# Attention in the layers' PSUM banks, scan turns placed ahead, and transposed copies written in runs of four words

## The chip, the cores and the metric

One core of one Trainium2 chip runs the whole program. The metric is the device time of one launch in microseconds (us): 1198.31 us is the median of 3 runs (1196.89 to 1199.21). Engines are named as in the profile: PE is TensorE (its weight loads are PEld), DVE is VectorE, ACT is ScalarE, POOL is GpSimd, SP is SyncE, which issues nearly all DMAs. Each engine works through its own queue in order. SBUF is the on-chip memory that all of them use; PSUM is the small memory into which PE writes, 8 banks of 128 partitions x 512 fp32 words.

## The reference

The input goes through a gated linear recurrence (called attention here) and then two feed-forward layers.

```python
# q, k, v, a_re, a_im: (4, 8, 768, 48); a is scaled to magnitude at most 0.999
for t in range(S):
    S_re, S_im = a_re*S_re - a_im*S_im + outer(k[t], v[t]), a_re*S_im + a_im*S_re
    y[t] = q[t] @ S_re
x = y as (3072 tokens, 384)
h = x @ w_in;   x = (h * clip(h + 3, 0, 6) / 6) @ w_out          # layer 1, d_ff 2048
h = x @ w_in2;  x = (max(h, 0) + alpha * min(h, 0)) @ w_out2     # layer 2, d_ff 2048
```

The weights arrive as 64-bit floats and are turned into pairs of fp32r words on the chip (DVE and ACT, lines 73 to 77, 293 and 294); each product of a layer is three fp32r matmuls.

## The kernel before

**Groups.** A group n is one batch and 256 of its 768 positions: two chunks (g = 0, 1) of 128 positions, all 8 heads. There are 12 groups, three per batch. Each has a normalisation (`norm_ops`), a scan (`scan_ops`), an attention (`attn_ops`, that is `chunk_ops` for each chunk) and `split_x`, which hands its result to the layers.

**Scan.** The cumulative products of the complex gates. DVE first runs along 8 steps within each of 128 partitions (lines 396 to 398). `totals` then copies the last step (ACT, tile `tot`, line 409), turns it with two PE transposes into the PSUM tile `ptt` (line 412) and copies it out to `bt` (ACT, line 413). On `bt` DVE runs four rounds of four small operations (429 to 432) and some twenty tiny ones (447 to 485). `back` turns the result with two transposes (`pe`, line 492) and one ACT copy (`EL`, line 495). DVE multiplies it in (508 to 510), and last come the scaled keys `Kt` and queries, which lie in place of `A` (518).

**Attention of a chunk.** Eight heads share a chunk, and its keys and queries, 96 values for each position, are turned so that the 96 are on the partitions. `tr` does that in four calls: `Kt` half 0, `Kt` half 1, queries half 0, half 1. A call is four PE transposes (line 566) into the PSUM tile `pt`, and one ACT copy (line 567) from there to `KT` or `QT`. Position 8t + j of a head lies at transpose j, column t, so the copy before reads 512 words in a row in PSUM and writes them 8 words apart:

```python
nc.scalar.copy(
    dst.rearrange("p h (t j) -> p j (h t)", j=J)[:, 4 * half : 4 * half + 4], pt[:D2])
```

`scores(i)` is one product for each of four heads (eight PE records of line 589) into `ps`, and one DVE multiply by the mask into `PT` (590). `outputs` adds the two products of four pairs of heads in `py` (624, 626), ACT copies it to `ys` (628), and six SP DMAs carry it to `xr`. `update` carries the state on: `pu` (599), a small product `gx` (601), then DVE and ACT on `W`.

**PSUM.** `ps1` has one buffer each of the tags `pt`, `ps` and `py`. `pt` serves `totals`, `back`, all `tr` calls and `gx`; `ps` serves both `scores` and `pu`. `psh` has two buffers of the tag `ph` (lines 649 on), in which the layers' first products land; `psf` has the three accumulators of the second products. That is all 8 banks.

**Layers.** `ffn` runs a layer over one or two groups, 16 blocks of 128 inner features each: `ain` (`ph`, line 658), `gate` (ACT and DVE, 670 to 680, result `gs`) and `bout` (`acc`, line 695).

**What sets the order.** The program text is produced by a list of positions written by hand: each step has a place on a made-up time axis (`tl.at`, `tl.stream`), and the operations of scan, attention and layers are interleaved by it. Group 0's attention has positions 46 to 56 and the first pass over group 0 starts at 58; group 1's attention has 110 to 122, between the end of that pass and the pass that starts at 122; group 2's scan has 152 to 190. The framework's scheduler then fills each engine's queue: among the instructions that are ready by its own timing model it takes the one that stands first in the text, and a tile gets a buffer when the one before it in that buffer is released. The queues are fixed before the program runs. `tc.high_priority(offset=n)` makes the instructions in it count as standing n places earlier.

Of the kernel before, what the change touches and what calls it, by code (L numbers as in the profile page):

```python
# [9 lines left out]
F32 = mybir.dt.float32  # L10
# [7 lines left out]

P = 128
NB = 1  # L20
WACT = 4
LAG = {1: 2, 2: 5}
NW = 15
# [2 lines left out]
C = 128  # L26
G = 2
GT = G * C
TB, J = 16, 8
# [190 lines left out]
def recurrence_ffn_kernel(ctx: ExitStack, tc, al, qkl, vl, w1, w2, alpha, q, k, v, a_re, a_im, out):  # L220
# [8 lines left out]
    D2 = 2 * D  # L229
# [10 lines left out]
    psh = main.enter_context(tc.tile_pool(name="psh", bufs=2, space=PSUM))  # L240
# [86 lines left out]
    ps1 = att.enter_context(tc.tile_pool(name="ps1", bufs=1, space=PSUM))  # L327
# [10 lines left out]
    def grp(n):  # L338
        return divmod(n, NG)
# [44 lines left out]
    def scan_ops(n):  # L384
# [4 lines left out]
        ops = []  # L389
# [15 lines left out]
        b2 = lp.tile([P, 2, H, TB], F32, tag="b2", name=f"b2_{n}")  # L405
        E = lp.tile([P, 2, H, TB], F32, tag="E", name=f"E{n}")

        def totals():
            nc.scalar.copy(tot[:, :, :, :D].rearrange("p c g d -> p g c d"), A[:, J - 1])
            pt = ps1.tile([P, 2, P], F32, tag="pt", name=f"ptt{n}")  # L410
            for c in range(2):
                nc.tensor.transpose(pt[:, c], tot[:, c].rearrange("p g d -> p (g d)"), ident)
            nc.scalar.copy(bt.rearrange("p c h t -> p c (h t)"), pt)

        ops.append(totals)
        for r in range(4):
            w = 1 << r
            xv = bt.rearrange("p c h (k w) -> p c (h k) w", w=2 * w)
# [24 lines left out]
        ph, phn = phi[n % 2], phi[(n + 1) % 2]  # L443
# [50 lines left out]
                )  # L494
            nc.scalar.copy(EL, pe_)

        ops.append(back)
        late = [lambda: V.scalar_tensor_tensor(gam, n2, SC, y1, op0=ALU.mult, op1=ALU.mult)]
        if cp_ < NG - 1:
            late += turn(phn[0:64], ph, 64)  # L500
# [3 lines left out]
        for g in range(G):  # L504
            X = A[:, :, g]
            x = X.rearrange("p j c d -> p j (c d)").unsqueeze(1).broadcast_to([P, 2, J, 2 * D])
# [4 lines left out]

        Kt = lp.tile([P, J, G, 2, D], F32, tag="Kt", name=f"Kt{n}", bufs=NB)
        Q_t[n], K_t[n] = A, Kt
# [27 lines left out]
    def attn_ops(n):  # L541
        xr = xr_t[n] = lp.tile([P, KT, GT], F32, tag="xr", name=f"xr{n}", bufs=2)
        return [op for g in range(G) for op in chunk_ops(n, g, xr)]
# [9 lines left out]
    def chunk_ops(n, g, xr):  # L553
        b, cp_ = grp(n)
        c = G * cp_ + g
        Qt, Kt, V = Q_t[n], K_t[n], V_t[n]
        QT = lp.tile([D2, H, C], F32, tag="QT", name=f"QT{n}_{g}", bufs=2)
        KTr = lp.tile([D2, H, C], F32, tag="KT", name=f"KT{n}_{g}")
        KN = lp.tile([P, H, D2], F32, tag="KN", name=f"KN{n}_{g}")
        PT = [lp.tile([P, 4, C], F32, tag="PT", name=f"PT{n}_{g}_{i}", bufs=2) for i in range(2)]  # L560
        ops = []

        def tr(src, dst, half):
            pt = ps1.tile([P, 4, P], F32, tag="pt", name=f"pt{n}_{g}_{half}")
            for jj in range(4):
                nc.tensor.transpose(pt[:D2, jj], src[:, 4 * half + jj, g].rearrange("p c d -> p (c d)"), ident)  # L566
            nc.scalar.copy(  # L567
                dst.rearrange("p h (t j) -> p j (h t)", j=J)[:, 4 * half : 4 * half + 4], pt[:D2]
            )

        def natural():
            if c < NCH - 1:
                for h in range(H):
                    nc.sync.dma_start(
                        KN[:, h],
                        Kt[TB * h : TB * (h + 1), :, g].rearrange("p j c d -> p j (c d)"),
                    )

        def kt0():
            natural()  # L580
            tr(Kt, KTr, 0)

        ops += [kt0, lambda: tr(Kt, KTr, 1), lambda: tr(Qt, QT, 0), lambda: tr(Qt, QT, 1)]

        def scores(i):
            ps = ps1.tile([P, 4, C], F32, tag="ps", name=f"ps{n}_{g}_{i}")
            for hh in range(4):
                h = 4 * i + hh
                nc.tensor.matmul(ps[:, hh], lhsT=KTr[:, h], rhs=QT[:, h], start=True, stop=True)  # L589
            nc.vector.tensor_mul(PT[i], ps, mask.unsqueeze(1).broadcast_to([P, 4, C]))  # L590

        ops += [lambda: scores(0), lambda: scores(1)]

        def update():
            if c == NCH - 1:
                return
            pu = ps1.tile([P, H, D], F32, tag="ps", name=f"pu{n}_{g}")
            for h in range(H):
                nc.tensor.matmul(pu[:D2, h], lhsT=KN[:, h], rhs=V[:, g, h], start=True, stop=True)  # L599
            gx = ps1.tile([P, H], F32, tag="pt", name=f"gx{n}_{g}")  # L600
            nc.tensor.matmul(
                gx[:D2], lhsT=sel[:, g].rearrange("p c d -> p (c d)"), rhs=gam_t[n], start=True, stop=True
            )
            W = lp.tile([D2, H, D], F32, tag="W", name=f"W{n}_{g}", bufs=2)
            gb = gx[:D2].unsqueeze(2).broadcast_to([D2, H, D])
            if c == 0:
                nc.scalar.copy(W, pu[:D2])
            else:
                nc.vector.tensor_add(W, W_t[n, g], pu[:D2])
            if n < WACT:  # L610
                gs_ = lp.tile([D2, H], F32, tag="gsb", name=f"gsb{n}_{g}")
                nc.scalar.copy(gs_, gx[:D2])
                for h in range(H):
                    nc.scalar.activation(W[:, h], W[:, h], AF.Copy, scale=gs_[:, h : h + 1])
            else:
                nc.vector.tensor_mul(W, W, gb)
            W_t[(n, 1) if g == 0 else (n + 1, 0)] = W

        def outputs():
            for hp in range(H // 2):  # L620
                for par in range(2):
                    h = 2 * hp + par
                    o = py[64 * par : 64 * par + D, hp]
                    nc.tensor.matmul(o, lhsT=V[:, g, h], rhs=PT[h // 4][:, h % 4], start=True, stop=(c == 0))  # L624
                    if c > 0:
                        nc.tensor.matmul(o, lhsT=W_t[n, g][:, h], rhs=QT[:, h], start=False, stop=True)  # L626
            ys = lp.tile([P, 4, C], F32, tag="ys", name=f"ys{n}_{g}")
            nc.scalar.copy(ys, py)
            tk = slice(g * C, (g + 1) * C)
            for par in range(2):  # L630
                nc.sync.dma_start(xr[D * par : D * (par + 1), :, tk], ys[64 * par : 64 * par + D, 0:3])
            for par, e0, kk, p0, m in ((0, 0, 0, 96, 32), (0, 32, 1, 96, 16), (1, 0, 1, 112, 16), (1, 16, 2, 96, 32)):
                nc.sync.dma_start(xr[p0 : p0 + m, kk, tk], ys[64 * par + e0 : 64 * par + e0 + m, 3])

        ops += [outputs, update]
        return ops
# [85 lines left out]
    def group(n, norm, scan, attn, split):  # L722
        tl.at(max(norm[0] - 8, 0.0), lambda: load_a(n))
        tl.stream(*norm, lambda: norm_ops(n))
        tl.at(scan[0] if n else 0.5, lambda: load_qk(n))
        tl.stream(*scan, lambda: scan_ops(n))
        tl.at(attn[0] - 6, lambda: load_v(n))
        tl.stream(*attn, lambda: attn_ops(n))
        tl.at(split, lambda: split_x(n))
# [13 lines left out]
    for m in range(2, NGRP // 2):  # L743
        if m + 1 < NGRP // 2:
            n = 2 * m + 2
# [103 lines left out]
```

## Time and profile before

| | |
|---|---|
| median of 3 runs | 1198.31 us |
| the profiled execution | 1198.93 us, span 1197.2 us |
| PE busy | 1031.2 us (86%) in 5914 matmuls |
| DVE busy | 802.1 us (67%) |
| ACT busy | 615.3 us (51%) |
| mean granted PE clock | 0.975 of full |
| DMA | 194.60 MB moved |

Busy is the time in which an engine had an instruction under way, and a share of the whole span. The program has two parts: some 400 us in which groups 0 to 5 are prepared while the weights are decoded, then a regular pattern of two groups at a time.

### The profile page before, as it was taken

Reading aid. Unit: us, or ns where it says so; the run is one execution under the profiler, and the core shown is the slowest. Engines: PE = TensorE matmul, PEld = TensorE weight load, DVE = VectorE, ACT = ScalarE, POOL = GpSimd, SP = SyncE. Lnnn points to the kernel's source line nnn. Section 1 sums busy time; section 2 is a strip of 40 time slices with the busy share of each in tenths; the row PEclk is TensorE's granted clock in tenths of the full one; section 3 lists DMA queues with packets and bytes.
Section 4 is the critical chain, followed back from the end, with each engine's and each line's share of the span. In section 5 each row is a group of like instructions: output and inputs, shape, how many; then the busy total and the mean of one; then the engine's idle time right before and its main releaser. Section 6 shows DMA issues by size and latency. Waiting matters only on the chain.

```text
span 1197.2 us, 15796 instructions
## 1 busy us (share of the span) xinstructions
PE 1031.2 (86%) x5914; PEld 846.9 (71%) x5914; DVE 802.1 (67%) x1537; ACT 615.3 (51%) x1003; POOL 2.0 (0%) x13
## 2 busy tenths in 40 slices
PE   0026946979998789999999999999999999999997
PEld 0015935957787787777878778778788777788786
DVE  7985973999895586948738749559579375333432
ACT  5453634667665455755356564446554346432433
POOL 0000000000000000000000000000000000000000
PEclk9999876999999899999999999999999999999999
DMA  8642472476575675445534544543454344244430
GB/s 339 253 167 61 142 303 67 134 275 194 222 247 181 213 243 178 134 128 174 171 102 153 171 120 158 193 136 116 131 188 139 130 124 138 89 163 134 133 129 30
DMA packets 70500, 194.60 MB, mean 163 GB/s; under 512 B 29456, under 2 KB 38672, under 8 KB 70416
## 3 DMA queue, kind: packets, MB, share of 16 engines
q1 hardware_dynamic: 70272, 193.50, 48.6%
q8 instruction: 49, 0.80, 0.3%
q14 instruction: 35, 0.29, 0.1%
q10 hardware_dynamic: 144, 0.01, 0.0%
HBM read 158.08 MB, written 22.81 MB: 151 GB/s over the span
## 4 chain that ended last, share of the span: by engine, by line
PE 66%; DVE 16%; ACT 12%; DMA 3%; issue 2%; SPq 0%; DVEq 0%; ACTq 0%
PE ph L658 27%; PE acc L695 24%; PE ps L589 5%; PE pt L566 4%; ACT KT L567 4%; ACT QT L567 4%; PE pu L599 3%; PE py L624 2%; DVE w L294 2%; DVE wd L76 2%; DVE wd L77 2%; PE py L626 2%; DMA w<-wsd 1%; DVE gs L680 1%; DMA A<-in_al_dram 1%
## 5 line engine op out<-in xcount | busy, mean ns | idle before, releaser
L695 PE MATMUL acc<-gs,w 128*128 128x512 f32 (+1 forms) x2016 | 453.3, 366 | 7.2 <-ACT gs L679 4.8
L695 PEld LDWEIGHTS acc<-gs,w 128*128 128x128 f32 x2016 | 335.2, 188 | 69.2 <-ACT gs L679 7.3
L658 PE MATMUL ph<-xT,w 128*128 128x256 f32 (+1 forms) x1152 | 231.2, 348 | 20.9 <-ACT xT L550 14.9
L658 PE MATMUL ph<-xs,w 128*128 128x512 f32 x864 | 224.3, 401 | 3.2 <-DVE xs L704 2.5
L658 PEld LDWEIGHTS ph<-xT,w 128*128 128x128 f32 x1152 | 185.1, 197 | 50.8 <-ACT xT L550 16.0
L658 PEld LDWEIGHTS ph<-xs,w 128*128 128x128 f32 x864 | 158.3, 188 | 40.6 <-DVE xs L704 4.0
L679 ACT CAST gs<-r 128x512 fp32r<-128x512 f32 x192 | 119.7, 624 | 119.6 <-DVE r L671 71.6
L680 DVE TENSOR_TENSOR gs<-r,gs 128x512 fp32r<-128x512 f32 x192 | 132.0, 689 | 63.5 <-ACT gs L679 63.4
L678 DVE SCALAR_TENSOR_TENSOR r<-n,nal,r 128x512 f32<-128x512 f32 x96 | 71.9, 749 | 80.9 <-ACT n L675 80.5
L670 ACT ACTIVATE r<-ph 128x512 f32<-128x512 f32 x96 | 57.3, 597 | 129.2 <-PE ph L658 128.7
L671 DVE SCALAR_TENSOR_TENSOR r<-r,ph 128x512 f32<-128x512 f32 x96 | 65.7, 684 | 83.4 <-ACT r L670 82.9
L674 ACT ACTIVATE r<-ph 128x512 f32<-128x512 f32 x96 | 57.5, 599 | 83.9 <-PE ph L658 83.1
L567 ACT COPY KT<-pt 96x512 f32<-96x512 f32 x48 | 54.8, 1143 | 47.6 <-PE pt L566 39.4
L590 DVE TENSOR_TENSOR PT<-ps,mask 128x512 f32<-128x512 f32 x48 | 33.2, 692 | 62.7 <-PE ps L589 61.0
L589 PEld LDWEIGHTS ps<-QT,KT 96*128 96x128 f32 x384 | 54.5, 214 | 21.8 <-ACT QT L567 18.5
L589 PE MATMUL ps<-QT,KT 96*128 96x128 f32 x384 | 60.5, 307 | 10.7 <-ACT QT L567 9.7
L567 ACT COPY QT<-pt 96x512 f32<-96x512 f32 x48 | 54.8, 1142 | 21.5 <-PE pt L566 21.5
L566 PE MATMUL pt<-ident,Kt 128*96 128x128 f32 x192 | 33.1, 298 | 38.0 <-DVE Kt L518 30.5
L675 ACT ACTIVATE n<-ph 128x512 f32<-128x512 f32 x96 | 57.4, 598 | 0.0
L566 PEld LDWEIGHTS pt<-ident,Kt 128*96 128x96 f32 x192 | 22.6, 136 | 48.6 <-ACT wd L73 21.2
L566 PE MATMUL pt<-ident,A 128*96 128x128 f32 x192 | 33.8, 303 | 20.9 <-ACT QT L567 10.3
L566 PEld LDWEIGHTS pt<-ident,A 128*96 128x96 f32 x192 | 20.9, 135 | 38.7 <-ACT QT L567 19.0
(107 smaller groups left out, 1054.0 us busy)
## 6 DMA issues: line engine op xcount, KB each, us to landing
w<-wsd SPq DMA_DIRECT2D x139, 768.0 KB, 4.4
raw<-in_w_dram SPq DMA_DIRECT2D x32, 768.0 KB, 5.7
wsd<-w SPq DMA_DIRECT2D x23, 768.0 KB, 4.1
A<-in_al_dram SPq DMA_DIRECT2D x12, 768.0 KB, 4.6
qk<-in_qkl_dram SPq DMA_DIRECT2D x12, 768.0 KB, 5.4
KN<-Kt SPq DMA_DIRECT2D x160, 48.0 KB, 2.3
v<-in_vl_dram SPq DMA_DIRECT2D x12, 384.0 KB, 4.4
out_dram<-o SPq DMA_DIRECT2D x18, 256.0 KB, 3.2
```

The costliest lines, as they stand in the source:

```text
L566: nc.tensor.transpose(pt[:D2, jj], src[:, 4 * half + jj, g].rearrange("p c d -> p (c d)"), ident)
L567: nc.scalar.copy(dst.rearrange("p h (t j) -> p j (h t)", j=J)[:, 4 * half : 4 * half + 4], pt[:D2])
L589: nc.tensor.matmul(ps[:, hh], lhsT=KTr[:, h], rhs=QT[:, h], start=True, stop=True)
L658: nc.tensor.matmul(ph_, lhsT=w[:, wl, kk], rhs=x[:, xl, kk], start=(kk == 0 and wl == 0 and xl == 0), stop=(kk == KT - 1 and wl == 1),)
L670: nc.scalar.activation(r, ph_, AF.Relu, bias=0.5, scale=1.0 / 6.0)
L671: nc.vector.scalar_tensor_tensor(r, r, 1.0, ph_, op0=ALU.min, op1=ALU.mult)
L674: nc.scalar.activation(r, ph_, AF.Relu)
L675: nc.scalar.activation(neg, ph_, AF.Relu, scale=-1.0)
L678: nc.vector.scalar_tensor_tensor(r[:, k], neg[:, k], nal[:, ii : ii + 1], r[:, k], op0=ALU.mult, op1=ALU.add)
L679: nc.scalar.copy(gs[:, 0], r)
L680: nc.vector.tensor_sub(gs[:, 1], r, gs[:, 0].bitcast(F32))
L695: nc.tensor.matmul(acc, lhsT=w[:, wl, e * P : (e + 1) * P], rhs=gs[:, gl], start=(i == 0 and wl == 0 and gl == 0), stop=(i == NF - 1 and g ...
```

## The change

Three edits.

1. In `tr` and `scores` of groups 0 and 1, some tiles come from the layers' two `ph` buffers: of the four `tr` calls of a chunk the second and third (`Kt` half 1, queries half 0), and of the two `scores` the second. The others stay in `pt` and `ps`.
2. For groups 0 to 3, `totals` and `back` are emitted with an offset of 1000 places ahead.
3. In all groups the copy out of `pt` goes over its 512 words in another order: it writes four neighbouring words of `KT` or `QT` at a time and reads them from the four transposes, 128 words apart in PSUM. The words and their places are the same.

```diff
+URGE = 1000
@@ scan_ops
+        def urgent(f):
+            def g():
+                with tc.high_priority(offset=URGE):
+                    f()
+            return g if n < 4 else f
+
-        ops.append(totals)
+        ops.append(urgent(totals))
...
-        ops.append(back)
+        ops.append(urgent(back))
@@ chunk_ops
+        def bank(k, own, name):
+            pool, tag = (psh, "ph") if n < 2 and k else (ps1, own)
+            return pool.tile([P, 4, P], F32, tag=tag, name=name)
+
         def tr(src, dst, half):
-            pt = ps1.tile([P, 4, P], F32, tag="pt", name=f"pt{n}_{g}_{half}")
+            pt = bank((src is Kt) == half, "pt", f"pt{n}_{g}_{half}")
             for jj in range(4):
                 nc.tensor.transpose(pt[:D2, jj], src[:, 4 * half + jj, g].rearrange("p c d -> p (c d)"), ident)
             nc.scalar.copy(
-                dst.rearrange("p h (t j) -> p j (h t)", j=J)[:, 4 * half : 4 * half + 4], pt[:D2]
+                dst.rearrange("p h (t j) -> p (h t) j", j=J)[:, :, 4 * half : 4 * half + 4],
+                pt[:D2].rearrange("p j x -> p x j"),
             )
...
         def scores(i):
-            ps = ps1.tile([P, 4, C], F32, tag="ps", name=f"ps{n}_{g}_{i}")
+            ps = bank(i, "ps", f"ps{n}_{g}_{i}")
```

## Rows read from the trace of the kernel before

**Rows 1.** Page: busy us (share of the span) and instructions of each engine.

```profile
PE 1031.2 (86%) x5914; PEld 846.9 (71%) x5914; DVE 802.1 (67%) x1537; ACT 615.3 (51%) x1003; POOL 2.0 (0%) x13
```

**Rows 2.** Page: chain of waits that ended last, share of the span by line.

```profile
PE ph L658 27%; PE acc L695 24%; PE ps L589 5%; PE pt L566 4%; ACT KT L567 4%; ACT QT L567 4%; PE pu L599 3%; PE py L624 2%; DVE w L294 2%; DVE wd L76 2%; DVE wd L77 2%; PE py L626 2%; DMA w<-wsd 1%; DVE gs L680 1%; DMA A<-in_al_dram 1%
```

**Rows 3.** Stretches: length, busy PE, PEld, DVE, ACT, POOL, PE clock, DMA share, GB/s.

```profile
121.00:158.00 37.00, 34.99 (x279) 34.17 (x279) 35.10 (x62) 20.63 (x33) 0.00 (x0) 0.93 0.53 197
...
169.00:211.00 42.00, 26.67 (x171) 22.19 (x172) 15.53 (x48) 18.30 (x38) 0.00 (x0) 0.62 0.30 76
...
240.00:270.00 30.00, 22.62 (x118) 17.39 (x117) 29.64 (x44) 19.41 (x29) 0.00 (x0) 1.00 0.77 274
...
406.00:1197.00 791.00, 766.42 (x4131) 618.24 (x4130) 481.88 (x912) 395.21 (x636) 0.00 (x0) 1.00 0.44 143
```

**Rows 4.** Groups by line: count, busy us, mean ns, idle before and releasers.

```profile
L567 ACT COPY KT<-pt 96x512 f32<-96x512 f32 x48 | 54.8, 1143 | 47.6 <-PE pt L566 39.4 <-PE ps L589 8.0
L567 ACT COPY QT<-pt 96x512 f32<-96x512 f32 x48 | 54.8, 1142 | 21.5 <-PE pt L566 21.5
...
L628 ACT COPY ys<-py 128x512 f32<-128x512 f32 x24 | 14.1, 587 | 33.7 <-PE py L626 26.0 <-PE py L624 5.6 <-DMA w<-wsd 1.8
```

**Rows 5.** Groups by line: three small DVE operations.

```profile
L466 DVE TENSOR_TENSOR pq<-phi,u 64x32 f32<-64x32 f32 x20 | 3.7, 186 | 0.3
...
L447 DVE TENSOR_TENSOR sq<-bt 128x16 f32<-128x16 f32 x12 | 2.2, 182 | 0.2
...
L448 DVE TENSOR_TENSOR n<-sq 128x8 f32<-128x8 f32 x12 | 2.0, 164 | 0.3
```

**Rows 6.** Timeline, group 0: start, length, instruction, [idle before and releaser].

```profile
79.35 1.10 ACT L567 COPY KT<-pt 96x512 f32<-96x512 f32 x1 [1.51 <-PE pt L566]
...
80.50 1.08 PE L566 MATMUL pt<-ident,Kt 128*96 128x128 f32 x4 [1.19 <-ACT KT L567]
...
120.35 0.80 PE L658 MATMUL ph<-xT,w 128*128 128x256 f32 x2 [5.43 <-ACT xT L550]
```

**Rows 7.** Who waited for line 567, 78 to 205 us: us, times.

```profile
  PE pt L566: 13.3, 11
...
  PE ps L589: 4.6, 4
```

**Rows 8.** Waits of DVE, 78 to 205 us: total, times, longest.

```profile
DVE PT L590 <- PE ps L589: 31.6, 7, 8.0
DVE W L609 <- PE pu L599: 9.5, 3, 4.2
```

**Rows 9.** Timeline, totals of group 2 during group 1's attention.

```profile
173.31 0.37 ACT L409 COPY tot<-A 128x192 f32<-128x192 f32 x1
...
196.39 0.69 PE L412 MATMUL ptt<-ident,tot 128*128 128x128 f32 x2 [0.31 <-ACT gsb L612]
```

**Rows 10.** Who waited for line 567, 406 to 1197 us: us, times.

```profile
  PEld pt L566: 27.1, 39
  PE pt L566: 10.0, 29
  PEld ps L589: 9.6, 13
  PE ps L589: 3.9, 10
```

**Rows 11.** Who waited for line 567, 211 to 406 us: us, times.

```profile
  PEld pt L566: 6.0, 9
...
  PEld ps L589: 2.5, 4
```

**Rows 12.** Timeline, a chunk in the regular part.

```profile
601.54 1.18 PE L695 MATMUL acc<-gs,w 128*128 128x512 f32 x4
...
603.13 0.64 PE L566 MATMUL pt<-ident,Kt 128*96 128x128 f32 x4 [0.41 <-ACT KT L567]
```

**Rows 13.** Chain in order of time: start, length, engine and line, count.

```profile
472.89 2.10 PE acc L695 x9
```

## The prediction, on record before the result

> **What bounds the kernel now.** I read the page's busy shares first, then the chain of waits, the stretches, and who waits for the copies of line 567. PE is busy for 86% of the span and no other engine for more than 67% [rows 1], so PE is the likely bound, but not everywhere. From 406 us on it is: 766 of 791 us busy [rows 3], and the missing 25 us are small holes. Before that the bound changes hands. In 121 to 158 us DVE is busy 35.1 of 37 us, in 240 to 270 us 29.6 of 30 while PE has 7.4 us of holes; in 169 to 211 us neither is full (PE 26.7, DVE 15.5, ACT 18.3 of 42) [rows 3]. There one hands to the other: four transposes fill the single `pt`, PE stands for 1.19 us while ACT copies it out in 1.10 us, and only then come the next four [rows 6]. DVE, which has other work, stands in its queue behind the masks of `scores` for 31.6 us and behind `pu` for 9.5 us of the first two attentions [rows 8]. The 96 copies of line 567, 54.8 + 54.8 us, lie on the chain with 4% + 4% of the span, some 90 us [rows 2, 4]: nearly all of them. That overstates what they cost, since PE works during much of a copy; the holes before the instructions that wait are the better measure.
>
> **Edit 3, the copy's price.** Today it reads 512 words in a row and writes them 8 words apart, in 1143 ns; the copy of `py`, as long and in a row on both sides, takes 587 ns [rows 4]. So scattered writing costs 556 ns, 1.09 ns a word. The new copy writes runs of four and reads words 128 apart. No ACT row reads PSUM in steps, so I bound it. Below: if only the writing was dear, 587 ns, as `py`. Above: line 447 reads DVE words 16 apart, 16 of them in 182 ns, where 8 in a row take 164 (line 448) and 32 take 186 (line 466), which puts 16 at some 171 [rows 5]; 11 ns for 16 words is 0.7 ns a word, and 512 words at that price make 587 + 358 = 945 ns; at the price of the scattered write it stays at 1143 ns. A dearer read than that (1.7 us at twice the price) I keep as the far end. I take 600 ns: the two copies of rows 4 differ in nothing but the order of the writes, which shows where the time sits, and the one hint at dear reads is another engine on another memory.
>
> The Trainium skill, page "Advanced Engine Details and Errata", sections "SBUF Cachelines" and "PSUM Cachelines", says that SBUF wants at least two hits on a line of 16 bytes, and that PSUM's lines hold two fp32 words and should be used in neighbouring pairs. Its first half agrees with 1143 against 587 ns; its second half, which it states for matmuls, speaks against this edit, and no row here shows it for an ACT read. Taken for ACT as well, it leaves the copy about where it is, which is the first rival below.
>
> **Edit 3, from 406 us on.** PE's loads stand before `pt` and `ps` 39 + 13 times for 27.1 + 9.6 us, 0.71 us each; by the matmul rows, whose ends are modelled late, it is 10.0 + 3.9 us [rows 10]. One example says which is nearer: four products start at 601.54, the transposes behind them at 603.13 [rows 12]; nine such products in a row take 2.10 us [rows 13], four therefore 0.93, so of the 1.59 us between the starts some 0.66 are hole. A copy 0.55 us shorter takes most of it: 52 holes x 0.48 = 25 us. Bounds: 14 us (the matmul rows' sum) and 29 us (52 x 0.55). Next late are then the matmuls themselves.
>
> **Edit 3, from 211 to 406 us.** 9 + 4 such holes, 6.0 + 2.5 us [rows 11]: 13 x 0.4 = 5 us, between 2 and 7, less where DVE is what ends last.
>
> **Edits 1 and 3, the first two attentions.** PE stands 13.3 + 4.6 = 18 us for line 567 here [rows 7]. With `pt`, `ph`, `ph` for the first three calls the transposes no longer wait for a copy; only the fourth call waits for the first copy, and each chunk's `scores` for the last. With copies of 0.60 us that leaves about 0.7 us for each of the four chunks: 18 - 3 = 15 us. With copies of 1.1 us ACT needs 4.4 us for what PE turns in 4.3 (four times 1.08 [rows 6]), so some 1.2 us are left for each: 18 - 5 = 13 us, which is edit 1 by itself. The second bank for `scores` I count at nothing, since rows 7 hold only waits for line 567; it can only add. The waits that edit 1 adds are free: the first product of a layer needs a `ph` buffer, but it comes at 120.35 us and waits 5.43 us for `xT` [rows 6], long after the last mask. Bounds of this term: 10 and 18 us. Whether the end of the attention moves the end of the kernel: the next stage needs `xT` from it, and DVE, the bound of 121 to 158 us, stood idle in the attention, so both move [rows 3, 8]. A plus that I leave out of the sum: the mean granted clock was 0.62 of full in 169 to 211 us [rows 3], a mix of the two levels (1.2 and 2.4 GHz) after a PE with holes; a denser PE may be given more.
>
> **Edit 2.** It moves seven instructions for each of four groups (`totals`: two ACT copies and two transposes; `back`: two transposes and one copy), no DMA, and nothing on SP or POOL. For group 0 nothing stands before them on PE. For group 2 it does: `tot` was copied at 173.31, its transposes came at 196.39, 22.7 us later, behind group 1's attention [rows 9]. Ahead of it they would give DVE the four rounds and the rest of the scan's small operations to run while it stands behind the masks, up to 8.0 us at a time [rows 8]. That saves nothing while DVE has slack, and something where DVE is the bound: at most the 7.4 us of PE's holes in 240 to 270 us [rows 3], and for group 1 the four rounds in 121 to 158 us, some 4 us (16 operations like those of rows 5 and somewhat longer). Price: each urgent pair takes `pt` and PE for 0.69 + 0.37 us and two hand-overs, some 1.3 us [rows 9], in the middle of an attention; four of them make 5 us at worst. Above: 12 us. I take 6 us, between -5 and 12.
>
> **Sum.** 25 + 5 + 15 + 6 = 51 us off the profiled execution's 1198.9 us: 1148 us. The median of the runs is 0.6 us less, which I neglect: 1148 us. Own range: 1134 to 1166.
>
> **Rivals.** First, the read is as dear as the write was: copies of 0.95 to 1.14 us. Only edits 1 and 2 are left, 13 + 6 = 19 us, and at 1.05 us some 0.1 us for each of 65 later holes, 6 us: 1174 us (1164 to 1182). For: line 447; against: the single cause that rows 4 suggest.
>
> Second, slower: a read in steps costs more than the scattered write did. All 96 copies pay, 65 holes grow later on and some 15 early. The point from which it decides: 19 us of gain over 80 holes is 0.24 us, so from copies of 1.38 us the kernel is slower. At twice the written price (1.7 us) it is 80 x 0.56 = 45 us: 1199 - 19 + 45 = 1225 us. Range 1202 to 1225. For: nothing but that no row has such a read. Against: the same.
>
> Third, the copies don't get shorter and the early gain is given back: DVE's decoding sets the start of the second layer, and the early attention only lengthens its wait: 1199 - 0 to 6, some 1196 us. For: DVE is full in 240 to 270 us. Against: 41 us of DVE's waits lie in the two attentions.
>
> Fourth, edit 2 doesn't do what it says: the urgent steps are not ready earlier in the scheduler's timing, or take `pt` at a bad moment. By itself 6 us less gain up to 11, so 1154 to 1159; it alone changes no sign, together with the first or third it may.
>
> **How the numbers follow.** Forecast 0.52 (with the fourth inside it), first rival 0.24, slower by dear reads 0.11, early gain given back 0.07, a reordered queue that costs more than the edits bring 0.06. The range goes from 1136 to 1196 us: above it lie the dear reads and most of the reordered queue, below it a few in a hundred. A change of 0.2% (2.4 us) is what a measurement can tell here. Faster: 0.52 + 0.24 + about half of 0.07 = 0.79; the same 0.05; slower 0.11 + 0.05 = 0.16.
>
> **What would show it.** Edit 3: line 567's mean, 0.6 against 1.0 to 1.14 or over 1.4 us, and with it the loads' waits after 406 us, 37 us now and under 12 if I am right. Edit 1: in the first attention four transposes follow each other without the 1.19 us, and the first layer product comes near 112 instead of 120.35 us. Edit 2: group 2's `ptt` some 20 us before the end of group 1's attention instead of behind it, and fewer than 7.4 us of PE holes in the stretch that answers to 240 to 270 us. Wrong I would be above all if line 567 stayed where it is, or if the first product came earlier and the stretch from there to 406 us grew by as much.

## The result, and the profile after

The changed kernel takes 1145.41 us (median of 4 runs, 1143.35 to 1145.79) against 1198.76 us: ratio 0.9555, 95% interval 0.9541 to 0.9569, 53 us less. 1148.0 had been forecast. The page of the kernel after, busy shares and the chain by engine and line:

```profile
PE 1017.0 (89%) x5914; PEld 849.2 (74%) x5914; DVE 799.7 (70%) x1537; ACT 565.3 (49%) x1003; POOL 2.0 (0%) x13
...
PE 77%; DVE 14%; ACT 4%; DMA 3%; issue 1%; SPq 0%; ACTq 0%; DVEq 0%
PE ph L671 31%; PE acc L708 30%; PE ps L602 5%; PE pt L578 3%; PE py L637 3%; PE pu L612 2%; DMA w<-wsd 2%; PE py L639 2%; DVE wd L77 2%; DVE w L295 1%; DVE wd L78 1%; DVE wd L75 1%; DVE r L684 1%; DVE gs L693 1%; DVE m L397 1%
```

ACT is busy 50 us less, and the copies (line 567 before, 579 now) are gone from the list of lines; they held 4% + 4% [rows 2]. The groups by line of the kernel after give the new price (mean ns after the comma):

```profile
L579 ACT COPY KT<-pt 96x512 f32<-96x512 f32 x48 | 28.0, 585 | 34.3 <-PE pt L578 32.3 <-PE ps L602 2.0
L579 ACT COPY QT<-pt 96x512 f32<-96x512 f32 x48 | 27.9, 587 | 14.0 <-PE pt L578 13.8
```

1143 ns [rows 4] became 586 ns, the price of the copy of `py`, which runs in a row on both sides. Who waited for it from 390 us on (us, times), in the kernel after:

```profile
  PEld pt L578: 5.8, 27
  PEld ps L602: 2.6, 10
  PEld ptt L419: 0.7, 3
```

The loads' 36.7 us before `pt` and `ps` [rows 10] fell to 8.4, and no matmul row waits for the copy any more (the last line, `ptt`, is not among [rows 10]; it was 2.4 us). In the first two attentions, 78 to 194 us of the kernel after, the same list reads:

```profile
  PEld ps L602: 6.1, 4
  PE ps L602: 4.8, 4
  PEld pt L578: 0.9, 2
  PE pt L578: 0.4, 1
```

The 11 transposes that stood for 13.3 us [rows 7] are down to one and 0.4 us; what stays is the wait of `scores` for the last copy of a chunk, 4.8 us where it was 4.6. DVE's waits there (total, times, longest) fell from 31.6 and 9.5 us [rows 8] to:

```profile
DVE PT L603 <- PE ps L602: 9.2, 7, 3.0
DVE W L622 <- PE pu L612: 3.6, 1, 3.6
```

The timeline of TensorE after, at the points where a stage begins:

```profile
78.49 1.91 PE L578 MATMUL pt<-ident,Kt 128*96 128x128 f32 x8 [20.85 <-DVE Kt L525]
...
109.19 0.80 PE L671 MATMUL ph<-xT,w 128*128 128x256 f32 x2 [5.18 <-ACT xT L557]
...
152.62 1.94 PE L578 MATMUL pt<-ident,Kt 128*96 128x128 f32 x8 [5.04 <-DVE Kt L525]
...
174.53 0.44 PE L419 MATMUL ptt<-ident,tot 128*128 128x128 f32 x2
...
376.19 8.58 PE L671 MATMUL ph<-xT,w 128*128 128x256 f32 x52 [0.30 <-DVE xT L558]
```

Eight transposes now follow each other where four stopped for 1.19 us [rows 6]. Such points place the gain. The table has, for every kernel with some of the edits, the start in us of four stages and the span of the same profiled execution; "third run" is the first long run of the third first-layer pass (the last row above), and the last column is what is left from there to the end. With edit 2 alone the second pass's long run is one record with the two products before it, some 1 us early. A row is a single execution: a second execution of the changed kernel has its first product 2.8 us earlier (the run with `back` urgent for two groups, below), so a step of 2 to 3 us in one row says little.

| kernel | first product | second attention | second pass's long run | third run | span | rest |
|---|---|---|---|---|---|---|
| before | 120.35 | 169.08 | 210.67 | 404.45 | 1197.2 | 792.8 |
| edit 1 alone | 114.01 | 162.91 | 200.97 | 404.27 | 1196.6 | 792.3 |
| edit 2 alone | 120.07 | 157.31 | 195.65 | 393.56 | 1185.4 | 791.8 |
| edit 3 alone | 115.25 | 163.63 | 201.88 | 391.00 | 1158.9 | 767.9 |
| 1 and 2 | 109.79 | 153.45 | 191.08 | 387.87 | 1179.4 | 791.5 |
| 1 and 3 | 108.76 | 157.19 | 191.76 | 386.22 | 1153.1 | 766.9 |
| 2 and 3 | 115.54 | 152.44 | 187.71 | 378.72 | 1146.0 | 767.3 |
| all (after) | 109.19 | 152.62 | 184.59 | 376.19 | 1143.5 | 767.3 |

The last column has two values only: 791.5 to 792.8 with the old copy, 766.9 to 767.9 with the new one. Some 25 us come from there, and 28.3 us from ahead of the third run. The old and the new copy are compared in pairs of kernels that differ in nothing else (before and edit 3 alone, for one), and in each pair every engine runs the same instructions in the same order, by line and tile: what edit 3 brings comes from the length of the copy alone. The stretch from the third run to the end, as a row of each kernel (length; busy PE, PEld, DVE, ACT, POOL; clock, DMA share, GB/s), first of before, then of after:

```profile
404.45:1197.20 792.75, 767.97 (x4136) 619.78 (x4136) 483.23 (x922) 395.31 (x636) 0.00 (x0) 1.00 0.44 144
```

```profile
376.19:1143.50 767.31, 758.24 (x4134) 621.01 (x4134) 477.89 (x903) 361.44 (x634) 0.00 (x0) 0.99 0.45 148
```

TensorE's holes fell from 24.8 to 9.1 us, 15.7 us. The other 9.7 us are busy time that vanished with nearly as many matmuls (4136 and 4134 records). The ends of matmuls are modelled in these profiles, so part of a hole may have been booked as a longer matmul; no row shows that directly. The loads' waits (28.3 us less) were nearer to the 25 us gained than the matmul rows' (13.9 us less, to nothing).

### The profile page after: what moved, and what is told of

It is laid out like the page before. It is cut to its first block, busy times and chain, and to the rows that moved or that the text cites. A ratio compares the mean times of both kernels' runs of the same rounds, so it can differ in the third digit from the quotient of the medians.

```text
span 1143.5 us, 15806 instructions
## 1 busy us (share of the span) xinstructions
PE 1017.0 (89%) x5914; PEld 849.2 (74%) x5914; DVE 799.7 (70%) x1537; ACT 565.3 (49%) x1003; POOL 2.0 (0%) x13
## 4 chain that ended last, share of the span: by engine, by line
PE 77%; DVE 14%; ACT 4%; DMA 3%; issue 1%; SPq 0%; ACTq 0%; DVEq 0%
PE ph L671 31%; PE acc L708 30%; PE ps L602 5%; PE pt L578 3%; PE py L637 3%; PE pu L612 2%; DMA w<-wsd 2%; PE py L639 2%; DVE wd L77 2%; DVE w L295 1%; DVE wd L78 1%; DVE wd L75 1%; DVE r L684 1%; DVE gs L693 1%; DVE m L397 1%
## 5 line engine op out<-in xcount | busy, mean ns | idle before, releaser
L397 DVE TENSOR_TENSOR m<-A 128x384 f32<-128x384 f32 x84 | 46.9, 558 | 1.9
L579 ACT COPY KT<-pt 96x512 f32<-96x512 f32 x48 | 28.0, 585 | 34.3 <-PE pt L578 32.3
L637 PE MATMUL py<-PT,v 128*48 128x128 f32 x384 | 42.0, 297 | 0.8 <-DVE PT L603 0.8
L515 DVE TENSOR_TENSOR Ts<-A,EL 128x1536 f32<-128x1536 f32 x24 | 42.1, 1754 | 0.1
```

What stands on the lines that cost most here:

```text
L397: ops.append((0.55, lambda: V.tensor_mul(m.rearrange("p g a c d -> p g a (c d)"), x, y)))
```

## The experiments

**Edit 3 alone.**

```diff
-            return g if n < 4 else f
+            return g if n < 0 else f
...
-            pool, tag = (psh, "ph") if n < 2 and k else (ps1, own)
+            pool, tag = (psh, "ph") if n < 0 and k else (ps1, own)
```

> Edit 3 alone (edits 1 and 2 undone). Theory (the copies' length is what PE waited for, in all groups): copies at 585 ns; the later terms of the prediction whole (25 + 5 us) and early 15 waits each shorter by some 0.55 us, 8 us: 1199 - 38 = 1161 us. Rival A (what counts after 406 us is only what the matmul rows show, 14 us, and the early part moves by the banks alone): about 1199 - 16 - 4 = 1179 us. Rival B (the queues' new order after edits 1 and 2 made the later gain): under 10 us, 1190 us.

1158.85 us, ratio 0.9676 (0.9652 to 0.97), 39 us: 25 in the last column, 8.8 up to the second pass, 4.7 from there to the third run. Each term is where the expectation put it.

**Edits 1 and 2 with the old copy.**

```diff
-                dst.rearrange("p h (t j) -> p (h t) j", j=J)[:, :, 4 * half : 4 * half + 4],
-                pt[:D2].rearrange("p j x -> p x j"),
+                dst.rearrange("p h (t j) -> p j (h t)", j=J)[:, 4 * half : 4 * half + 4], pt[:D2]
```

> Edits 1 and 2 with the old order of the copy. Theory: copies at 1140 ns, the later holes as before (37 us of the loads' waits), the early part shorter by 13 + 6 us: 1180 us; stretch from the second pass's first product to the end as long as before within 3 us. Rival (without short copies the early gain is given back by DVE's decoding): 1195 to 1199 us.

1182.18 us, 0.9879 (0.986 to 0.9897): 16 us, of which the last column shows 1.3. The copies took 1149 ns.

**Edits 1 and 3, without the urgent turns** (the first pair of lines of the first experiment).

> The whole change but edit 2. Theory: edit 2 was worth 6 us, so 1151 us; without it the transposes of group 2's totals stand behind group 1's attention. Rival A: the banks alone already bring the totals forward, edit 2 is worth nothing: 1145 us. Rival B: the urgent steps cost the attention more than they bring: 1142 us or less.

1153.3 us, 0.9633 (0.9619 to 0.9647). Edit 2 is worth 8 us beside the others, and the table shows its place: without it the first product comes at the same time, the second attention 4.6 us later, the second pass 7.2 and the third run 10.0 us later.

**Edits 2 and 3, without the banks** (the second pair of lines).

> The whole change but edit 1. Theory: with copies at 585 ns the single bank still holds PE for about 0.6 us per call, the banks save 15 - 8 = 7 us: 1152 us, and four transposes, copy, four transposes alternate again at the start of group 0's attention. Rival: short copies leave nothing for the banks to save: 1146 us.

1146.71 us, 0.9577 (0.9558 to 0.9595): edit 1 is worth 1 to 3 us beside both others, not 7. That is the rival's number, but not its reason: the banks still save 6.35 us up to the first product. The timeline of TensorE in this kernel:

```profile
115.54 0.80 PE L671 MATMUL ph<-xT,w 128*128 128x256 f32 x2 [5.63 <-ACT xT L557]
...
152.44 0.64 PE L578 MATMUL pt<-ident,Kt 128*96 128x128 f32 x4 [1.63 <-DVE Kt L525]
```

Without the banks the layers begin 6.35 us later, and yet the second attention begins at the same 152.5 us. What lies between is in the chain of the kernel after (start, length, engine and line), from 119 us on:

```profile
118.89 0.60 DVE r L684
119.48 0.47 DVE A L516
...
120.61 0.60 DVE gs L693
...
121.68 0.87 DVE w L295
```

It goes on like this: gates, weights, scan and decoding on one queue, DVE, up to 139 us. The stretch from the first product to the second attention, of the kernel after and then without the banks:

```profile
109.19:152.62 43.43, 37.01 (x291) 35.59 (x291) 40.38 (x71) 26.21 (x43) 0.00 (x0) 0.93 0.63 241
```

```profile
115.54:152.44 36.90, 34.68 (x273) 33.41 (x273) 36.25 (x54) 23.15 (x36) 0.00 (x0) 0.92 0.53 193
```

DVE is nearly full in both, and TensorE, which starts earlier with the banks, stands 6.4 us instead of 2.2. So beside edit 2 the lead is used up on DVE before the second attention begins.

**Edit 1 alone, and edit 2 alone** (the copy's diff, with either line of the first experiment).

> Edit 1 alone (old copy, no urgent turns). Theory of the prediction: 13 us, 1186 us. Newer theory, after the runs so far (DVE, the bound between the first attention's end and the second's start, gives part of it back): the first attention ends some 9 us earlier than before, the second starts at most 5 us earlier: 1188 to 1192 us. Rival: the old copies leave ACT the bound of the attention, 1195 us.

> Edit 2 alone. Prediction: 6 us, 1193 us. Newer theory (beside the short copies edit 2 was worth 12 us without the banks and 8 us with them, since it hands DVE work while it stands in the attentions): 10 to 12 us, 1187 us. Rival (the urgent steps hold the only pt while copies are long, and the attention pays): 1198 us or slower.

Edit 1: 1195.01 us, 0.9966 (0.9954 to 0.9978), 4 us. The newer theory (1188 to 1192) missed; the rival's number came, but not for its reason, since the attentions did get shorter. The kernel was 9.7 us ahead at the second pass and 0.2 us at the third run. (This execution was the longest of its eleven, 1198.31 us, so it may show some 3 us more loss than the median run.) The stretches that answer to each other, first with edit 1 alone, then before:

```profile
200.00:240.00 40.00, 37.48 (x294) 36.12 (x293) 34.41 (x63) 20.60 (x33) 0.00 (x0) 0.92 0.49 167
240.00:300.00 60.00, 47.05 (x233) 35.29 (x233) 56.76 (x80) 39.89 (x64) 0.00 (x0) 0.89 0.57 201
```

```profile
210.00:250.00 40.00, 37.13 (x293) 35.75 (x292) 37.98 (x55) 24.57 (x39) 0.00 (x0) 0.94 0.55 185
250.00:310.00 60.00, 52.95 (x302) 40.09 (x301) 55.20 (x80) 43.62 (x69) 0.00 (x0) 1.00 0.67 229
```

With edit 1 alone DVE has more room in the first stretch (34.4 of 40 us busy against 38.0) and is nearly full in the second, where TensorE stands 13 us instead of 7; the granted clock there is 0.89 against 1.00. What moved is work of group 2's scan. Its factors `E` are ready at 201.3 us with edit 1 alone and at 209.8 before. Timeline of TensorE, their turn, with edit 1 alone and then before:

```profile
207.36 0.27 PE L499 MATMUL pe<-ident,E 128*128 128x128 f32 x1
...
237.05 0.27 PE L499 MATMUL pe<-ident,E 128*128 128x128 f32 x1
```

```profile
209.61 0.69 PE L492 MATMUL pe<-ident,E 128*128 128x128 f32 x2
```

The second transpose of the turn stands 36 us among the second pass's products. DVE's work that hangs on it (some 9.5 us: the multiplications by the factors and the scales of the keys) begins at 245.67 instead of 212.12 us, in the stretch that decoding fills. With edits 1 and 3 it is the same (factors at 192.1, second transpose at 227.14 us). From the second pass to the third run edit 1 adds 9.5 us by itself and 5.3 beside edit 3, but no more than 0.6 beside edit 2, with which group 2's turn follows its factors at once (182.65 us in the kernel after). No run moves this one turn by itself.

Edit 2: 1186.28 us, 0.9893 (0.9876 to 0.9911), 12.7 us, more than the forecast gave it. It comes from a wait that I had not read. Timeline of before, group 1's factors `E` and their turn:

```profile
125.02 0.28 DVE L485 TENSOR_TENSOR E<-b,b 128x120 f32<-128x120 f32 x1
...
147.22 0.38 PE L492 MATMUL pe<-ident,E 128*128 128x128 f32 x2
```

Timeline with edit 2 alone:

```profile
121.70 0.28 DVE L491 TENSOR_TENSOR E<-b,b 128x120 f32<-128x120 f32 x1
...
122.13 0.66 PE L499 MATMUL pe<-ident,E 128*128 128x128 f32 x2
...
157.31 0.64 PE L578 MATMUL pt<-ident,Kt 128*96 128x128 f32 x4 [1.65 <-DVE Kt L525]
```

In before the turn stood 22 us behind the first pass's products in TensorE's queue. It waited for nothing that a row calls a wait: the row has no bracket, since TensorE was busy. The rest of group 1's scan hung on it, and with it the second attention, 11.8 us earlier here.

**Copies of one kernel in six orders.** The changed kernel, but in groups 7 to 11 the copy goes over its words in five other orders; the calls are left out here and the comments say what each does. It leaves out the right places of the words in groups 9 to 11.

```diff
+ if n == 7:    # writes runs of two, reads 128 apart
+ elif n == 8:  # writes single words 8 apart, reads in a row
+ elif n == 9:  # writes in a row, reads 128 apart
+ elif n == 10: # in a row on both sides
+ elif n == 11: # writes 8 apart, reads 4 apart
  else:         # runs of four, as in the changed kernel
```

> The copy of line 567 in six forms, one per group from group 6 on, read as mean durations. It leaves out the right places of the words in KT and QT for groups 9 to 11. Group 6: runs of four written, read 128 words apart. 7: runs of two written, read 128 apart. 8: single words written 8 apart, read in a row. 9: written in a row, read 128 apart. 10: a row on both sides. 11: single words written 8 apart and read 4 apart. Theory (the price is a write that finds no second word in its 16-byte stretch; reads in steps are free): 585, 585, 1150, 585, 585, 1150 ns. Rival A (each jump of the writing costs): 585, 865, 1150, 585, 585, 1150. Rival B (reads in steps cost too, hidden so far beside the writing): group 11 over 1400, or group 9 over 650 ns.

One run, 1151.7 us. Groups by line, of groups 7, 8, 9, 10, 11 and the others in this order:

```profile
L583 ACT COPY KT<-pt 96x512 f32<-96x512 f32 x4 | 2.7, 668 | 3.1 <-PE pt L578 3.1
...
L588 ACT COPY KT<-pt 96x512 f32<-96x512 f32 x4 | 4.6, 1158 | 4.8 <-PE pt L578 4.8
...
L590 ACT COPY KT<-pt 96x512 f32<-96x512 f32 x4 | 2.3, 584 | 2.1 <-PE pt L578 2.1
...
L592 ACT COPY KT<-pt 96x512 f32<-96x512 f32 x4 | 2.3, 580 | 4.5 <-PE pt L578 4.5
...
L594 ACT COPY KT<-pt 96x512 f32<-96x512 f32 x4 | 4.7, 1176 | 1.7 <-PE pt L578 1.6
...
L596 ACT COPY KT<-pt 96x512 f32<-96x512 f32 x28 | 16.3, 584 | 18.3 <-PE pt L578 16.3 <-PE ps L616 2.0
```

Reading 128 words apart costs nothing (584 against 580 ns), and 4 apart next to nothing beside dear writes (1176 against 1158). The whole price is in the writes: single words 8 apart double the copy, runs of two cost 88 ns more than a row, where 0 had been expected, and runs of four 4. The Trainium skill, page "Advanced Engine Details and Errata", section "SBUF Cachelines", asks for at least two hits on a line of 16 bytes: with two the copy is nearly at full speed here, with four entirely. Its section "PSUM Cachelines" wants neighbouring pairs, for matmuls; for ACT's read this run measures no such price.

**One decoding step on POOL.** If DVE is the bound between the attentions, its work elsewhere should show it.

```diff
-        nc.vector.tensor_sub(wt[:, 1], t, wt[:, 0].bitcast(F32))
+        nc.gpsimd.tensor_sub(wt[:, 1], t, wt[:, 0].bitcast(F32))
```

> The changed kernel with the last subtraction of the weights' decoding (32 of some 0.96 us, 24 of them in the first 250 us) moved from DVE to POOL, which is idle. Theory (DVE is the bound from the first attention's end to the second's start): DVE has 23 us less to do there and in the first 78 us; 8 to 15 us faster than the changed kernel, 1131 to 1138 us. Rival A (PE and the chain through the attention are the bound): 1145 us. Rival B (POOL is slow, or holds up DVE while it reads SBUF): DVE's operations get longer, 1145 to 1170 us.

1176.94 us, 0.9823 (0.9806 to 0.9841), 31 us slower than the changed kernel. Groups by line of this kernel:

```profile
L295 POOL TENSOR_TENSOR w<-wd,w 128x768 fp32r<-128x768 f32 x32 | 89.0, 2781 | 248.4 <-ACT w L294 191.3 <-DVE r L684 52.4 <-DMA raw<-in_w_dram 4.7
L77 DVE SCALAR_TENSOR_TENSOR wd<-raw,wd 128x768 int32<-128x768 int32 x32 | 37.2, 1163 | 0.0
```

The step takes 2781 ns instead of 960, and DVE's own step beside it 1163 instead of 960; the first attention starts at 98.80 us instead of 78.49. This tells nothing of the question, since the next weight waits for POOL: ACT's first step of the decoding stands 48.7 us for it.

**A shorter decoding, with and without the banks.** The last of DVE's four decoding steps is left out, and with it the lowest three bits of each weight.

```diff
-    V.scalar_tensor_tensor(b, lo, 29, b, op0=ALU.logical_shift_right, op1=ALU.bitwise_or)
```

> The changed kernel with the last of VectorE's four decoding operations left out (it leaves out the lowest three bits of every weight): 32 operations of 0.95 us less on VectorE, 16 of them in the first pass and 16 in the second. Taken together with the next run. Theory (VectorE's decoding bounds the stretches after the first two attentions, and therefore gives back what the extra banks gain): with less decoding VectorE is late less often, this kernel takes 1133 to 1142 us, and it stands 4 to 7 us ahead of its twin without the banks. Rival (the gain is given back elsewhere, by TensorE's order or by the wait for the next group's scan): the two stand 1 to 3 us apart, as with the whole decoding (1.3 us), and the time is 1143 to 1146.

> Edits 2 and 3 without edit 1, with the same operation of the decoding left out. Theory: 1138 to 1148, 4 to 7 us behind its twin with the banks. Rival: 1 to 3 us behind it.

1126.88 us, 0.9387 (0.9364 to 0.941), and 1129.65 us, 0.942 (0.9407 to 0.9433). Timeline, the third run, with the banks and then without:

```profile
360.33 7.53 PE L670 MATMUL ph<-xT,w 128*128 128x256 f32 x52 [2.23 <-DVE xT L557]
```

```profile
362.41 7.75 PE L670 MATMUL ph<-xT,w 128*128 128x256 f32 x52 [2.27 <-DVE xT L557]
```

Both halves of the expectation missed. Of the 30.7 us of DVE work left out (32 steps of 959 ns), 16 are gained at the third run with or without the banks, 13 of them behind the start of the second pass: about half of the work left out was on the path up to there, more than the theory said. But the two kernels stand 2.8 us apart, where 4 to 7 had been expected; the rival's size was right. DVE is not free even so: between the first product and the second attention it is busy 40.7 of 41.2 us with the banks and 35.6 of 36.6 without. The pair is a weak test of what becomes of a lead, since the banks bring the first product only 1.3 us forward here (109.49 and 110.76 us), and the second attention comes later with them (150.68 and 147.44). At 1127 us it is the fastest kernel here, at the price of three bits.

**`back` urgent for two groups only.**

```diff
-        def urgent(f):
+        def urgent(f, top=4):
...
-            return g if n < 4 else f
+            return g if n < top else f
...
-        ops.append(urgent(back))
+        ops.append(urgent(back, 2))
```

> The changed kernel, but the step that turns the factors back (`back`) goes ahead in the queue for groups 0 and 1 alone; `totals` still does for the first four. In the changed kernel TensorE stands 3.6 us and 5.8 us before the turns of groups 2 and 3, since they were put ahead of products that were ready. Theory (those stands are a loss, and the scans of groups 2 and 3 aren't late without it): 1137 to 1143 us. Rival (the early turn of groups 2 and 3 is what brings their attention forward, as it does for group 1): 1146 to 1152.

1143.54 us, 0.9544 (0.953 to 0.9558). Neither theory was tested: the queues of all engines are, instruction by instruction (line and tile), those of the changed kernel. For groups 2 and 3 the offset of `back` moves nothing. The stand of 3.6 us ahead of group 2's turn stays without it; the one of 5.8 us was misread, for it lies ahead of the fifth turn (374.81 us), that of a group beyond the first four, to which no kernel gives an offset; group 3's turn (322.58 us) stood 0.6. So this is a second measurement of the changed kernel, 1.9 us from the first. The two profiled executions part in one place, the first attention: the sixteen products of the first `scores` took 3.78 us in the changed kernel's and 2.05 in this one. The rows give a granted clock of 1.00 for both, but the first clock record of the two traces is at 87.8 and at 81.3 us, so for the slower products (from 83.15 us) there is none. The second chunk's sixteen products take 3.78 us in both executions, at a granted 0.50, the lower level (1.2 GHz). So the slower products fit that level; no record shows it.

**`back` urgent for group 1 alone, no `totals`.**

```diff
-            return g if n < 4 else f
+            return g if n == 1 else f
...
-        ops.append(urgent(totals))
+        ops.append(totals)
```

> The changed kernel with edit 2 cut down to one step: `back` of group 1 goes ahead in the queue, no `totals` does, and no other group's `back`. Theory (nearly all of edit 2's gain beside the others, 8 us, comes from `back` of group 1, which had waited some 22 us on TensorE behind the first pass's products): 1143 to 1148 us, with group 1's `pe` within 2 us of its factors and the second attention near 153 us. Rival (the early totals, group 2's above all, carry it, as the prediction had it): 1150 to 1154, as without edit 2.

1147.5 us, 0.959 (0.957 to 0.9609), as the theory had it. Timeline of this kernel, and then without edit 2:

```profile
110.86 0.45 PE L499 MATMUL pe<-ident,E 128*128 128x128 f32 x1 [0.47 <-DVE E L491]
...
150.43 1.87 PE L578 MATMUL pt<-ident,Kt 128*96 128x128 f32 x8 [5.03 <-DVE Kt L525]
```

```profile
135.34 0.38 PE L499 MATMUL pe<-ident,E 128*128 128x128 f32 x2
...
157.19 1.91 PE L578 MATMUL pt<-ident,Kt 128*96 128x128 f32 x8 [9.61 <-DVE Kt L525]
```

One step of one group, two transposes and a copy, brings 5.8 of the 8 us. The rest is 2 to 4 us by the two measurements of the changed kernel, and its ratios (0.9541 to 0.9569, 0.953 to 0.9558) lie below this one's. The timeline of this kernel shows where it may lie:

```profile
218.06 0.38 PE L499 MATMUL pe<-ident,E 128*128 128x128 f32 x2
```

Group 2's turn stands 34 us behind its factors, which are ready at 183.8 us, just after the second pass began; in the changed kernel it comes with them, just ahead of that pass. From the second pass to the third run this kernel takes 195.5 us, the changed one 191.6. With `back` urgent for two groups the turn came in time without an offset of its own, so by these two runs it is the early totals that put it there. That this is worth the difference is read from the timelines, not shown by a run.

## Why the prediction was right, and where it was not

**Edit 3's price was right, by the reason given.** 586 ns against the 600 taken; the six orders show that nothing but the scattered write had been dear, as the two copies of [rows 4] suggested. Line 447, on which the upper bound and the first rival rested, was DVE reading SBUF and said nothing of ACT reading PSUM. The dear read fell with it.

**Edit 3, 25 + 5 us, was right.** 25 us in the last column of the table and 4.7 us between the second pass and the third run, with edit 3 alone. The sizing by 0.48 us of each load's wait, checked on the starts of two rows, held; the matmul rows' 14 us would have been little more than half.

**"Edits 1 and 3, the first two attentions: 15 us" was about right as a sum, and wrong in its parts.** With both, 18.2 us are gained at the third run, of which 4.7 belong to the term before. But "13 us, which is edit 1 by itself" is the step that failed: alone it gave 4 us, beside edit 2 2 to 4, beside edit 3 some 5.5, beside both 1 to 3. Its local part came as forecast (first product at 109.19, near the 112 foretold). The step from there, that "both move" because DVE stood idle in the attention, was wrong, in a different place with and without edit 2. With edit 2, the second attention starts when DVE's full queue has come to its keys, and TensorE's earlier start only lengthens its wait for DVE. Without edit 2, the lead reaches the second pass (9.7 us with edit 1 alone) and is lost behind it, where group 2's turn is late and its scan falls into DVE's full stretch. Both are the third rival's mechanism, the early gain given back to DVE, for the one edit; I had given it 0.07, as a fate of the early gain as a whole. Edit 3 alone already brought 8.8 us of that stretch. The plus that was left out, the clock, is small where it can be read: 0.62 in the second attention of before, 0.71 in that of the kernel after (152.62 to 184.59 us).

**"Edit 2: 6 us, between -5 and 12" was too small.** It is 12.7 us alone, 8 beside the others. The forecast looked for a step that waited behind an attention, and found group 2's totals [rows 9]; these moved from 23 to 6 us behind their copy, some 4 us before the end of group 1's attention (179.1 us) rather than the 20 foretold, and they may hold the smaller part of the gain. The step that mattered most was group 1's `back`, 22 us behind the products. The price of "four of them", 5 us, was not paid as such: for groups 2 and 3 the offset of `back` moved nothing.

**The sum** (51 forecast, 53 measured) is so near partly by luck. Taken by edits, the forecast has 32 us for edit 3 (25 + 5, and the 2 that it adds to the 13), 13 for edit 1 and 6 for edit 2; alone they gave 39, 4 and 12.7. Edit 1 was 9 us too much, the other two 7 us too little each, and together the three bring 2 to 3 us less than their single gains (56). Two of the signs foretold came: loads' waits under 12 us (8.4), and holes in the stretch that answers to 240 to 270 us under 7.4; it reads, in the kernel after:

```profile
214.00:244.00 30.00, 26.82 (x168) 22.19 (x167) 29.66 (x46) 21.35 (x34) 0.00 (x0) 1.00 0.82 294
```

3.2 us of holes, with DVE as full as before (29.66 of 30). A sign of being wrong came too, for edit 1 alone: an earlier first product, and a stretch from there to the third run that grew by nearly as much (284.1 us before, 290.3 with it).

## What to carry to other kernels

A step that stands in a full engine's queue shows no idle time, and so no view of waits names it: look for the instruction whose input was ready long before it began, here two transposes 22 us late, with most of edit 2's gain behind them. A gain inside a stage counts only as far as the next bound lets it through: ask what the next stage waits for, and whether that engine is full. A lead can also move a third step to a bad place in a queue, as group 2's turn, so the queues have to be read again after the change. And when a copy rearranges data, put the steps on the side where they are free, which a row of the same copy in a plain order tells beforehand.

## What the runs showed of the hardware

ACT reads PSUM in steps of 128 words at no price (584 against 580 ns for 512 words), while writes of single words 8 apart take 1158 ns and runs of two 668. The same subtraction of 128 x 768 words takes 2781 ns on POOL and 960 on DVE, and DVE's two-input step on other data grows from 960 to 1163 ns while POOL works; the Trainium skill, page "Advanced Engine Details and Errata", section "VectorE Performance Modes", says that VectorE's second SBUF port is shared with GpSimd, and that GpSimd's instructions and VectorE's two-port ones get in each other's way; these rows agree that DVE slows beside POOL, but do not show through which port.
